# Attention and two feed-forward layers on one core: place of the scale products, tiles of the last weight load, shape of the last job

## The chip, the cores and the metric

The kernel runs on one core of one Trainium2 chip. The metric is the device time of one execution in microseconds; lower is better. Three runs of the kernel before were timed, and one more execution was profiled.

## The reference, cut to what matters

```python
mask = q_bucket[:, :, :, None] == k_bucket[:, :, None, :]      # 2 x 8 heads, 768 tokens, 64 wide
scores = np.where(mask, scale * q @ k.T, -1e9)
attn = softmax(scores)
x = (attn @ v)                       # as 1536 tokens x 512
p = domain_probs / domain_probs.sum(-1)
for e in range(4):                   # first feed-forward: 4 experts, 512 -> 1024 -> 512
    out += p[:, e:e+1] * (np.maximum(x @ w1[e], 0) @ w2[e])
h = out @ w_in                       # second feed-forward: 512 -> 2048 -> 512
g = np.where(h >= 1, h, np.where(h <= -1, 0, (h + 1) ** 2 / 4))
return g @ w_out
```

## The kernel before, in words

**Units of work.** Each expert is cut into two halves of 512 hidden columns, which gives the weight blocks u = 0 to 7; the second feed-forward has four such blocks, u = 8 to 11. A block has four chunks f of 128 hidden columns, for each of its two matrices (kind 1 and kind 2). A job is a pair of a block and a group of token tiles (128 tokens each). Its first layer makes 12 products per chunk into one PSUM tile; its second layer makes three products per chunk and token tile into one PSUM tile per token tile. Each operand is held as a high and a low half, so every product is made three times.

**First stage.** The attention is cut into 96 units, and 17 jobs on the first six token tiles (`JOBS_A`, L45) run between them. The list scheduler `Order` (L61 to L283) sets the order of this stage: every step has a cost, a due time and the buffers that it uses, and the scheduler writes out one order for all engines. `fill` (L893) lists the job steps. For each of the 52 weight chunks of either kind it has a load (`ldw`, `w_dma`, L803), on SP or on ACT's queue, whichever the scheduler finds free; a conversion on ACT (`whi`, L832); and two low halves on POOL or DVE (`wlo`, L836). A chunk is loaded into a raw tile, of which there are two for each kind (`raw_n`, L296), so chunk s can't be loaded before the low halves of chunk s - 2 are made. The last eight chunks (block 1, four of each kind) are converted here but used in the second stage. Where the scheduler foresees idle time on PE it puts in products on a dummy tile (`warm`, L1040), so many as fit. In one place of the stage the scale of block 0 is found: PE turns a column of maxima (L406), DVE takes four small steps (L394 to L404), PE spreads the result (L411).

**Second stage.** After `S.run` the attention's pools are closed (`attx.close()`), and new pools take their memory. From there the order is that of the code. The loop at the end makes, for each job and chunk, `l1b` (L1313) of the next job, one pending transposition of x (`x_all`), `step` (L1432), `l2b` (L1400) of this job, and `step` again. There are two PSUM tiles for the first layer (`mm_tile`), so a first layer waits for all readers of the tile two before it. `step` moves the generators on: loads that are due (`fetch_w`), scaling and conversion of weights (`w_steps`, `conv_w`), the scan of x after the first feed-forward (`x2_steps`), and the unpacking of the second feed-forward's weights (`w64_steps`). All of SP's loads in this stage are in one queue, in order; the first of them (L1193, L1195) stand at its start.

**Scale products.** A scale is found in `fin` (L1083): a maximum on DVE, a turn on PE, four steps on DVE (L1094 to L1097), a spread on PE, two steps on DVE (L1107, L1108). The two PE steps ride in the free columns 384 to 511 of a first-layer tile (`rider`, L1065), and `rest()` is the DVE part that reads them. In `l1b` `rest()` is the last thing.

**Blocks 8 to 11.** The first layer's result goes through two activations on ACT (L1350, L1351; the first tile is `ga`, the second `gg`), a product on DVE (L1352), a sum on POOL (L1353) and then `halves` (L1357 on ACT, L1358 on DVE). `halves` of a chunk is put off to the next chunk (`halve`, `split`). The activations need five small factors per token group, which `scales2` (L1296) makes in five DVE steps; it is called in `l1b` itself, at f = 0. The factors need the scale of the group's x (`e2`) and those of both weight matrices.

**The end.** `l2b_last` (L1414) makes the second layer of the last job: it first lets `split` make the last halves, then goes through the three token tiles one by one, with chunks 0 to 3 each, and each tile's sum goes to DVE (L1391) and out on SP (L1396).

Of the kernel before, what the change touches and what calls it, by code (L numbers as in the profile page):

```python
# [286 lines left out]
def attn_moe_kernel(ctx: ExitStack, tc, q, k, v, proj, probs, w1, w2, w_in, w_out, out):  # L287
# [510 lines left out]
    NCH = 4 * len(loads)  # L798
    wt = {1: {}, 2: {}}
# [4 lines left out]
    def w_dma(kind, s, e):  # L804
        if s >= NCH:
            return
        nxt_dma[kind] = s + 1
        u, f = loads[s // 4], s % 4
        if u >= 8:
            return  # L810
        t = raw[kind][s] = raw_p.tile([128, 512], F32, tag=f"raw{kind}", name=f"raw{kind}", bufs=raw_n[kind])
        if kind == 1:
            src = w1[u // 2]
            f0 = (u % 2) * 512
            src = src[:, f0 + f * 128:f0 + f * 128 + 128].rearrange("(c p) f -> p c f", p=128)
            e.dma_start(t.rearrange("p (c f) -> p c f", c=KC), src)
        else:
            src = w2[u // 2]
            f0 = (u % 2) * 512 + f * 128
            e.dma_start(t, src[f0:f0 + 128, :])  # L820
# [72 lines left out]
    def fill():  # L893

        NA = 4 * (job_load[len(JOBS_A) - 1] + 2)
        wb = {}
        half_raw = {}
        for s in range(NA):
            for kind in (1, 2):
                br = S.buf(f"raw{kind}", 2)  # L900
# [56 lines left out]
    with tc.manual_schedule():  # L957
# [347 lines left out]

        def grp(j):
            return jobs[j][1][0] // 3
# [5 lines left out]
        def l1b(j, f):  # L1313
# [26 lines left out]
            if u < 8:  # L1340
                act.activation(gg[:, 0:n], ps[:, 0:n], AF.Relu, scale=2.0 ** -15)  # L1341
                act.activation(hh[:, 0:n], gg[:, 0:n], AF.Copy)  # L1342
                dve.tensor_tensor(hl[:, 0:n], gg[:, 0:n], hh[:, 0:n], ALU.subtract)  # L1343
            else:
                need(2, u)
                if f == 0 and (u == 8 or grp(j) == 0):
                    scales2(u, slice(grp(j), grp(j) + 1) if u == 8 else slice(0, 4))
# [5 lines left out]
                pool.tensor_tensor(gg[:, 0:n], gg[:, 0:n], a[:, 0:n], ALU.add)  # L1353
                split()
# [6 lines left out]
            rest()  # L1361

        def l2b_mm(j, i, f, o):
            if j < JF:
                l2_mm(j, i, f, o)
                return
            whi, wlo = w16[2, jobs[j][0], f]
            hh, hl = hts[j, f]
            ts = slice(i * 128, i * 128 + 128)
            pe.matmul(o, hh[:, ts], whi, start=(f == 0), stop=False)  # L1370
            pe.matmul(o, hh[:, ts], wlo, start=False, stop=False)  # L1371
            pe.matmul(o, hl[:, ts], whi, start=False, stop=(f == 3))  # L1372

        def l2b_ev(j, i, o):
            u, tts = jobs[j]
            tt = tts[i]
            if j < JF:
                l2_ev(j, i, o)
            elif u < 8:
                sc = prk[u][:, tt:tt + 1]  # L1380
                if tt not in started:
                    started.add(tt)
                    dve.tensor_scalar(acc[tt], o, sc, None, ALU.mult)
                else:
                    dve.scalar_tensor_tensor(acc[tt], o, sc, acc[tt], ALU.mult, ALU.add)
            else:
                ko = k5[u][:, 4, grp(j):grp(j) + 1]
                if u == 8:
                    act.activation(acc[tt], o, AF.Copy, scale=ko)
                else:  # L1390
                    dve.scalar_tensor_tensor(acc[tt], o, ko, acc[tt], ALU.mult, ALU.add)  # L1391
            if u == 11:
# [4 lines left out]
                    out[r0:r0 + 128 * n, :].rearrange("(t c) d -> t c d", c=n)[:, tt - TT0[g]], acc[tt]  # L1397
# [16 lines left out]
        def l2b_last(j):  # L1414
            split()
            for i in range(len(jobs[j][1])):
                o = ps_m.tile([128, DM], F32, tag=f"o{i}", name=f"o{i}")
                for f in range(4):
                    l2b_mm(j, i, f, o)
                l2b_ev(j, i, o)  # L1420

        def x2_steps(tts):
# [7 lines left out]
            turn.extend((tt, s2[:, c]) for tt in tts)  # L1430

        def step(j):  # L1432
# [7 lines left out]
            for kind in (1, 2):  # L1440
                next(wgen[kind], None)
            if j > JF:
# [55 lines left out]
```

## Time and profile before

| what | value |
|---|---|
| runs | 1015.18, 1015.7, 1019.3 us; median 1015.7 |
| the profiled execution | 1014.5 us, of which the span on the core is 1012.4 |
| PE busy, in the span | 955.4 us (94%) |
| DVE, ACT, POOL busy | 724.2, 728.3, 360.4 us |
| granted TensorE clock, mean | 0.987 |
| chain that ended last | PE 67%, DVE 11%, ACT 10%, DMA 8% |

The span is cut by the order of the program: to about 423 us the first stage, from there the second, in which the second feed-forward begins at about 733 us. The time outside the span (2.1 us) is that of the start and the end of an execution. PE's busy time counts modelled ends of products that overlap, so idle time counts only from where the pipe has run empty.

### The profile page before, as it was taken

The page shows a single profiled execution, that of the slowest core. Times are in us where ns is not written, and L with a number is a line of the kernel's source. Part 1 is how long each engine was busy: PE and PEld are TensorE (multiplying, and loading weights), DVE is VectorE, ACT ScalarE, POOL GpSimd, SP SyncE. Part 2 cuts the span into 40 slices and gives each one's busy share as a digit, 9 for nine tenths or more (in the row PEclk, how much of TensorE's full clock was granted, in tenths as well). Part 3 has the DMA queues.
Part 4 walks back from the last instruction along what each step waited for, and adds up shares of the span by engine and source line. Part 5 has one row for each costly group of instructions (what it writes and reads, how often), then busy time and mean ns, then how long its engine had stood idle before and what let it go on. Part 6 is the DMA issues. An engine that isn't in the chain of part 4 may idle for free.

```text
span 1012.4 us, 19329 instructions
## 1 busy us (share of the span) xinstructions
PE 955.4 (94%) x6847; PEld 614.8 (61%) x6847; DVE 724.2 (72%) x1932; ACT 728.3 (72%) x1574; POOL 360.4 (36%) x397
## 2 busy tenths in 40 slices
PE   5568999999999999899999999999998999999998
PEld 2246888787888789785555555555544555555553
DVE  6998988899888884447665756655677777774654
ACT  6888897889888884357786777767776785656442
POOL 0332555554645654505110111104241353434221
PEclk9879999999999999999999999999999999999999
DMA  9799999999999885352433333110110111100012
GB/s 225 170 217 189 215 223 237 235 229 198 191 231 204 179 184 123 117 165 62 147 108 101 125 105 104 42 42 22 42 42 22 43 42 53 32 1 1 1 44 82
DMA packets 254753, 121.35 MB, mean 120 GB/s; under 512 B 180736, under 2 KB 239424, under 8 KB 254656
## 3 DMA queue, kind: packets, MB, share of 16 engines
q1 hardware_dynamic: 251296, 117.50, 49.4%
q10 hardware_dynamic: 3360, 2.62, 0.9%
q8 instruction: 53, 0.87, 0.4%
q14 instruction: 44, 0.36, 0.1%
HBM read 70.28 MB, written 3.15 MB: 73 GB/s over the span
## 4 chain that ended last, share of the span: by engine, by line
PE 67%; DVE 11%; ACT 10%; DMA 8%; issue 3%; SPq 1%; POOL 0%; ACTq 0%; DVEq 0%; POOLq 0%
PE mm L1334 7%; PE mm L1335 7%; PE mm L1336 7%; PE o L1370 6%; PE o L1372 6%; PE o L1371 6%; PE s L636 4%; DMA pt<-pn 3%; PE m L868 3%; DMA raw<-in_moe_w_dram 3%; PE m L850 3%; PE m L851 3%; PE m L852 3%; PE m L870 3%; PE m L869 3%
## 5 line engine op out<-in xcount | busy, mean ns | idle before, releaser
L686 POOL TENSOR_TENSOR pn<-e,pn 128x192 f16<-128x192 f32 (+3 forms) x165 | 138.3, 843 | 193.9 <-ACT pn L678 49.1
L1353 POOL TENSOR_TENSOR gg<-gg,ga 128x384 f32<-128x384 f32 x64 | 70.3, 1099 | 153.8 <-DVE ga L1352 150.5
L1343 DVE TENSOR_TENSOR hl<-gg,hh 128x384 f16<-128x384 f32 x72 | 42.9, 596 | 82.1 <-ACT hh L1342 82.0
L658 DVE CUSTOM_DVE_ANT_0 e<-s,mk,sc 128x768 f32<-128x768 f32 x96 | 96.9, 1010 | 2.3 <-ACT acc L716 0.6
L636 PE MATMUL s<-xk,xq 128*128 128x384 f16 (+1 forms) x384 | 81.7, 337 | 13.6 <-DVE usm L658 9.7
L1350 ACT ACTIVATE ga<-mm,half,k 128x384 f32<-128x384 f32 x64 | 42.6, 666 | 68.2 <-PE mm L1336 46.8
L850 PE MATMUL m<-x0h,w1h 128*128 128x256 f32 x304 | 91.5, 301 | 0.0
L671 ACT ACTIVATE e<-e,usm 128x768 f32<-128x768 f32 x96 | 89.3, 930 | 1.9 <-ACT acc L716 0.2
L851 PE MATMUL m<-x0l,w1h 128*128 128x256 f32 x304 | 86.1, 283 | 0.2 <-DVE sc L530 0.2
L852 PE MATMUL m<-x0h,w1l 128*128 128x256 f32 x304 | 86.0, 283 | 0.0
L678 ACT ACTIVATE pn<-e 128x768 f16<-128x768 f32 (+3 forms) x104 | 81.7, 786 | 4.6 <-DMA pt<-pn 4.4
L1352 DVE SCALAR_TENSOR_TENSOR ga<-ga 128x384 f32<-128x384 f32 x64 | 38.5, 601 | 62.8 <-ACT ga L1350 62.8
L1372 PE MATMUL o<-w2l,hl 128*128 128x512 f16 x216 | 82.0, 379 | 1.1 <-DVE hl L1358 1.1
L1370 PE MATMUL o<-w2l,hh 128*128 128x512 f16 x216 | 82.1, 380 | 0.0
L1371 PE MATMUL o<-w2l,hh 128*128 128x512 f16 x216 | 82.0, 379 | 0.0
L1358 DVE SCALAR_TENSOR_TENSOR hl<-gg,k,hh 128x384 f16<-128x384 f32 x64 | 59.9, 936 | 20.7 <-ACT hh L1357 20.5
L1370 PE MATMUL o<-w2h,hh 128*128 128x512 f16 x192 | 73.0, 380 | 0.0
L1372 PE MATMUL o<-w2h,hl 128*128 128x512 f16 x192 | 72.9, 379 | 0.0
L1371 PE MATMUL o<-w2h,hh 128*128 128x512 f16 x192 | 72.8, 379 | 0.0
L1372 PEld LDWEIGHTS <-hl 128*128 128x128 f16 x408 | 39.9, 98 | 49.7 <-DVE hl L1358 1.6
L1341 ACT ACTIVATE gg<-mm 128x384 f32<-128x384 f32 x72 | 34.7, 483 | 46.2 <-PE mm L1104 21.9
L868 PE MATMUL m<-w2h,hh 128*128 128x512 f32 x152 | 65.0, 428 | 0.0
(258 smaller groups left out, 2934.4 us busy)
## 6 DMA issues: line engine op xcount, KB each, us to landing
raw<-in_moe_w_dram SPq DMA_DIRECT2D x126, 256.0 KB, 3.4
r<-in_moe_w_in_dram SPq DMA_DIRECT2D x16, 512.0 KB, 3.7
r<-in_moe_w_out_dram SPq DMA_DIRECT2D x16, 512.0 KB, 3.5
rawx<-in_moe_w_dram SPq DMA_DIRECT2D x24, 256.0 KB, 3.9
out_dram<-acc SPq DMA_DIRECT2D x12, 256.0 KB, 2.0
raw<-in_moe_w_dram ACTq DMA_DIRECT2D x10, 256.0 KB, 3.0
w<-in_moe_w_dram SPq DMA_DIRECT2D x8, 256.0 KB, 5.2
rk<-in_k_dram SPq DMA_DIRECT2D x5, 384.0 KB, 3.8
```

What stands on the lines that cost most here:

```text
L636: pe.matmul(sps[:, j, 0:n], st["xq"][1 - i][:, hh * QG[pgs[m][0]][2] + c], st["x"][:, hh, 384 * j:384 * j + n], start=(i == 0), stop=(i == 1))
L658: dve.tensor_tensor_reduce(out=e.rearrange("p (a b) -> p a b", a=2), in0=u["s"][:, :, 0:384], in1=u["mk"].rearrange("p (a b) -> p a b", a= ...
L671: act.activation(u["e"], u["e"], AF.Exp, scale=-1.0, bias=sm[:, 2:3], accum_out=sm[:, 3:4])
L678: act.activation(u["pn"][:, c0:c1], u["e"][:, c0:c1], AF.Copy)
L686: eng[e].tensor_tensor(u["pn"][:, 768 + c0:768 + c1], u["e"][:, c0:c1], u["pn"][:, c0:c1], ALU.subtract)
L850: pe.matmul(ps[:, 0:n], hi[:, ws], xh[:, kc, xs], start=(kc == 0), stop=False)
L851: pe.matmul(ps[:, 0:n], hi[:, ws], xl[:, kc, xs], start=False, stop=False)
L852: pe.matmul(ps[:, 0:n], lo[:, ws], xh[:, kc, xs], start=False, stop=(kc == KC - 1))
L868: pe.matmul(o, hh[:, ts], whi, start=(f == 0), stop=False)
L1370: pe.matmul(o, hh[:, ts], whi, start=(f == 0), stop=False)
L1371: pe.matmul(o, hh[:, ts], wlo, start=False, stop=False)
L1372: pe.matmul(o, hl[:, ts], whi, start=False, stop=(f == 3))
```

## The change

There are four parts. In `fill` and `w_dma`, the last two chunks of each kind (s = 50 and 51) are loaded into tiles of the pool that held raw keys, values and queries (`rk`, `rv`, `rq`), under the scheduler's rules for these tags. In `l1b`, `rest()` stands right behind the first activation for blocks below 8, and behind the sum on POOL, ahead of `split`, for the others. The factors are made by a new function `factors`, called where the scan of x ends and in every `step`, as soon as their inputs are there, no more in `l1b`. In `l2b_last`, the first two token tiles go through chunks 0 to 2 before either goes through chunk 3, and the third token tile is made, evicted and sent in two halves of 256 columns.

```diff
--- before.py
+++ after.py
@@ -796,6 +796,8 @@
         job_load.append(len(loads) - 1)
         job_last.append(j == len(jobs) - 1 or jobs[j + 1][0] != u)
     NCH = 4 * len(loads)
+    NA = 4 * (job_load[len(JOBS_A) - 1] + 2)
+    EXTRA = {NA - 2: (("rk", 1), ("rq", 2)), NA - 1: (("rv", 1), ("rq", 2))}
     wt = {1: {}, 2: {}}
     raw = {1: {}, 2: {}}
     done_w = {1: 0, 2: 0}
@@ -808,7 +810,15 @@
         u, f = loads[s // 4], s % 4
         if u >= 8:
             return
-        t = raw[kind][s] = raw_p.tile([128, 512], F32, tag=f"raw{kind}", name=f"raw{kind}", bufs=raw_n[kind])
+        if s in EXTRA:
+            tag, n = EXTRA[s][kind - 1]
+            if n == 1:
+                t = flat(rq_p.tile([128, 2, 6, D], F32, tag=tag, name=tag, bufs=1))[:, 0:512]
+            else:
+                t = flat(rq_p.tile([128, 12, D], F32, tag=tag, name=tag, bufs=2))[:, 0:512]
+            raw[kind][s] = t
+        else:
+            t = raw[kind][s] = raw_p.tile([128, 512], F32, tag=f"raw{kind}", name=f"raw{kind}", bufs=raw_n[kind])
         if kind == 1:
             src = w1[u // 2]
             f0 = (u % 2) * 512
@@ -892,12 +902,11 @@
 
     def fill():
 
-        NA = 4 * (job_load[len(JOBS_A) - 1] + 2)
         wb = {}
         half_raw = {}
         for s in range(NA):
             for kind in (1, 2):
-                br = S.buf(f"raw{kind}", 2)
+                br = S.buf(*EXTRA[s][kind - 1]) if s in EXTRA else S.buf(f"raw{kind}", 2)
                 load(f"ldw{kind}.{s}", 0.73, lambda e, kind=kind, s=s: w_dma(kind, s, e), lambda cur: cur + K_LDW, w=[f"raw{kind}.{s}"],
                      use=[br], act_too=True, gate=4)
                 if s // 4 == NA0 + NA1 - 1:
@@ -1303,6 +1312,16 @@
             dve.reciprocal(cc, gp)
             dve.tensor_scalar(ko, gp, ew[2, u], None, ALU.mult)
 
+        have, e2_done = set(), set()
+
+        def factors(u, g):
+            if (u, g) in have or (1, u) not in scaled or (2, u) not in scaled:
+                return
+            gs = {g} if u == 8 else set(range(4))
+            if gs <= e2_done:
+                have.update((u, i) for i in gs)
+                scales2(u, slice(g, g + 1) if u == 8 else slice(0, 4))
+
         def grp(j):
             return jobs[j][1][0] // 3
 
@@ -1339,18 +1358,20 @@
             gg = g_p.tile([128, 384], F32, tag="gg", name="gg")
             if u < 8:
                 act.activation(gg[:, 0:n], ps[:, 0:n], AF.Relu, scale=2.0 ** -15)
+                rest()
                 act.activation(hh[:, 0:n], gg[:, 0:n], AF.Copy)
                 dve.tensor_tensor(hl[:, 0:n], gg[:, 0:n], hh[:, 0:n], ALU.subtract)
             else:
                 need(2, u)
-                if f == 0 and (u == 8 or grp(j) == 0):
-                    scales2(u, slice(grp(j), grp(j) + 1) if u == 8 else slice(0, 4))
+                factors(u, grp(j))
+                assert (u, grp(j)) in have
                 k2, kh, gp, cc, ko = (k5[u][:, i, grp(j):grp(j) + 1] for i in range(5))
                 a = g_p.tile([128, 384], F32, tag="ga", name="ga")
                 act.activation(a[:, 0:n], ps[:, 0:n], AF.Relu, bias=half, scale=kh)
                 act.activation(gg[:, 0:n], ps[:, 0:n], AF.Relu, bias=nhalf, scale=kh)
                 dve.scalar_tensor_tensor(a[:, 0:n], a[:, 0:n], 1.0, a[:, 0:n], ALU.min, ALU.mult)
                 pool.tensor_tensor(gg[:, 0:n], gg[:, 0:n], a[:, 0:n], ALU.add)
+                rest()
                 split()
 
                 def halves():
@@ -1358,20 +1379,19 @@
                     dve.scalar_tensor_tensor(hl[:, 0:n], gg[:, 0:n], cc, hh[:, 0:n], ALU.mult, ALU.subtract)
 
                 halve.append(halves)
-            rest()
-
-        def l2b_mm(j, i, f, o):
+
+        def l2b_mm(j, i, f, o, cs=slice(0, DM)):
             if j < JF:
                 l2_mm(j, i, f, o)
                 return
             whi, wlo = w16[2, jobs[j][0], f]
             hh, hl = hts[j, f]
             ts = slice(i * 128, i * 128 + 128)
-            pe.matmul(o, hh[:, ts], whi, start=(f == 0), stop=False)
-            pe.matmul(o, hh[:, ts], wlo, start=False, stop=False)
-            pe.matmul(o, hl[:, ts], whi, start=False, stop=(f == 3))
-
-        def l2b_ev(j, i, o):
+            pe.matmul(o, hh[:, ts], whi[:, cs], start=(f == 0), stop=False)
+            pe.matmul(o, hh[:, ts], wlo[:, cs], start=False, stop=False)
+            pe.matmul(o, hl[:, ts], whi[:, cs], start=False, stop=(f == 3))
+
+        def l2b_ev(j, i, o, cs=slice(0, DM)):
             u, tts = jobs[j]
             tt = tts[i]
             if j < JF:
@@ -1388,13 +1408,13 @@
                 if u == 8:
                     act.activation(acc[tt], o, AF.Copy, scale=ko)
                 else:
-                    dve.scalar_tensor_tensor(acc[tt], o, ko, acc[tt], ALU.mult, ALU.add)
+                    dve.scalar_tensor_tensor(acc[tt][:, cs], o, ko, acc[tt][:, cs], ALU.mult, ALU.add)
             if u == 11:
                 g = 0 if tt < 2 else (1 if tt < 6 else 2)
                 b, t0, n = QG[g]
                 r0 = b * S_ + t0
                 sp.dma_start(
-                    out[r0:r0 + 128 * n, :].rearrange("(t c) d -> t c d", c=n)[:, tt - TT0[g]], acc[tt]
+                    out[r0:r0 + 128 * n, :].rearrange("(t c) d -> t c d", c=n)[:, tt - TT0[g], cs], acc[tt][:, cs]
                 )
 
         def l2b(j, f):
@@ -1413,11 +1433,19 @@
 
         def l2b_last(j):
             split()
-            for i in range(len(jobs[j][1])):
-                o = ps_m.tile([128, DM], F32, tag=f"o{i}", name=f"o{i}")
+            u, tts = jobs[j]
+            o = [ps_m.tile([128, DM], F32, tag=f"o{i}", name=f"o{i}") for i in range(2)]
+            for i in range(2):
+                for f in range(3):
+                    l2b_mm(j, i, f, o[i])
+            for i in range(2):
+                l2b_mm(j, i, 3, o[i])
+                l2b_ev(j, i, o[i])
+            for h in range(2):
+                o = ps_m.tile([128, DM], F32, tag=f"o{2 * h}", name=f"o{2 * h}")
                 for f in range(4):
-                    l2b_mm(j, i, f, o)
-                l2b_ev(j, i, o)
+                    l2b_mm(j, 2, f, o[:, 0:256], slice(256 * h, 256 * h + 256))
+                l2b_ev(j, 2, o[:, 0:256], slice(256 * h, 256 * h + 256))
 
         def x2_steps(tts):
             g = tts[0] // 3
@@ -1428,6 +1456,8 @@
                 yield
             yield from fin(am, 3, e2[:, c], s2[:, c], 1)
             turn.extend((tt, s2[:, c]) for tt in tts)
+            e2_done.add(g)
+            factors(8, g)
 
         def step(j):
             for x in late:
@@ -1439,6 +1469,9 @@
             x2q[:] = [x for x in x2q if next(x, "end") != "end"]
             for kind in (1, 2):
                 next(wgen[kind], None)
+            for u in range(8, 12):
+                for g in range(4):
+                    factors(u, g)
             if j > JF:
                 w64_step()
 
```

The new order, where it matters below (line numbers of the new kernel stand 9 to 40 above those of the old one). First, ACT at the end of the first stage; `w1h` and `w2h` are the conversions of weight chunks, `hh<-mm` the first eviction of the second stage. Before:

```order
L832 ACTIVATE w1h<-raw_7500 128x512
L832 ACTIVATE w2h<-raw_7405 128x512
L832 ACTIVATE w2h<-raw_7413 128x512
L820 DMA raw_7553<-in_moe_w_dram 128x512
L832 ACTIVATE w2h<-raw_7550 128x512
L832 ACTIVATE w2h<-raw_7553 128x512
L857 ACTIVATE hh<-mm 128x256 x5
```

and now:

```order
L842 ACTIVATE w1h<-rv 128x512
L867 ACTIVATE hh<-m 128x256
L842 ACTIVATE w2h<-raw_7418 128x512
L842 ACTIVATE w2h<-raw_7437 128x512
L842 ACTIVATE w2h<-rq 128x512 x2
L867 ACTIVATE hh<-mm 128x256 x5
```

The load that stood between the conversions is gone from here, and the last two read a query tile.

Second, PE where the scale of block 0 is found in the first stage (`mx_w` is turned, `dmxw` is spread). Before:

```order
L406 MATMUL m<-ident,mx_w 2x128
L868 MATMUL m<-w2h,hh 128x512
L869 MATMUL m<-w2l,hh 128x512
L870 MATMUL m<-w2h,hl 128x512
...
L411 LDWEIGHTS ones
L411 MATMUL m<-dmxw,ones 128x2
```

and now:

```order
L406 MATMUL m<-ident,mx_w 2x128
L1049 LDWEIGHTS warm
L1049 MATMUL mm<-warm 128x256
...
L411 LDWEIGHTS ones
L411 MATMUL m<-dmxw,ones 128x2
L878 MATMUL m<-w2h,hh 128x512
```

Between the turn and the spread stood nine second-layer products; now six dummy products stand there, and the second layer comes behind the spread.

Third, DVE at the second token group of block 8 (`e` is the scale of x, `k` the factors, `mt` the first step on the next ridden product). Before:

```order
L1352 SCALAR_TENSOR_TENSOR ga<-ga 128x384
L1358 SCALAR_TENSOR_TENSOR hl<-gg,k_11111,hh 128x384
L1107 COPY e_7612<-mm 128x1
...
L1385 SCALAR_TENSOR_TENSOR acc<-o_11137,prk,acc 128x512
L1300 TENSOR_SCALAR k_11111<-e_7612,ew_8_10405 128x1
...
L1352 SCALAR_TENSOR_TENSOR ga<-ga 128x384
L1358 SCALAR_TENSOR_TENSOR hl<-gg,k_11111,hh 128x384
L1094 TENSOR_REDUCE mt<-mm 1x1
```

and now:

```order
L1372 SCALAR_TENSOR_TENSOR ga<-ga 128x384
L1116 COPY e_7614<-mm 128x1
L1117 RECIPROCAL s_7615<-mm 128x1
L1379 SCALAR_TENSOR_TENSOR hl<-gg,k_10883,hh 128x384
L1309 TENSOR_SCALAR k_10883<-e_7614,ew_8_10407 128x1
...
L1405 SCALAR_TENSOR_TENSOR acc<-o_11144,prk,acc 128x512
L1372 SCALAR_TENSOR_TENSOR ga<-ga 128x384
L1103 TENSOR_REDUCE mt<-mm 1x1
```

The copy of the scale moved ahead of the low half `hl`, the factors ahead of the three evictions `acc`, and the next ridden product's first step ahead of its `hl`. On SP, the loads of chunks 50 and 51 moved forward among the attention's transposes, and the order of the first stage differs on every engine from about SP's 177th row on. SP's first load of the second stage, which waited for no engine, now waits for POOL's last low half, because its tile lies over the query tiles.

## Rows read from the trace of the kernel before

**Rows 1.** Windows, by stage: PE, PEld, DVE, ACT, POOL busy us (instructions), clock, DMA, GB/s

```profile
290.00:423.00 133.00, 132.90 (x1259) 111.89 (x1257) 94.09 (x292) 95.92 (x227) 73.09 (x98) 1.00 0.77 163
423.00:437.00 14.00, 9.66 (x64) 9.33 (x65) 5.24 (x20) 3.08 (x8) 4.98 (x8) 0.88 0.93 299
...
700.00:800.00 100.00, 92.98 (x515) 49.35 (x514) 69.72 (x164) 71.12 (x143) 28.73 (x26) 1.00 0.13 40
```

**Rows 2.** Waits of PE, 395 to 450 us: total us, times, longest

```profile
PE mm L850 <- DVE hl L862: 3.6, 1, 3.6
PE mm L850 <- DVE acc L880: 0.8, 1, 0.8
```

**Rows 3.** Timeline of ACT at the end of the first stage: start, duration, what

```profile
424.51 0.35 ACTq L820 DMA_DIRECT2D raw<-in_moe_w_dram  x1
...
429.06 0.63 ACT L832 ACTIVATE w2h<-raw 128x512 fp32r<-128x512 f32 x1 [1.93 <-DMA raw<-in_moe_w_dram]
429.59 0.64 ACT L857 ACTIVATE hh<-mm 128x256 fp32r<-128x256 f32 x2
```

**Rows 4.** Timeline of POOL there

```profile
421.66 2.82 POOL L836 TENSOR_TENSOR w2l<-raw,w2h 128x256 fp32r<-128x256 f32 x4 [0.56 <-ACT w2h L832]
```

**Rows 5.** Timeline of DVE there: one step beside POOL's work, and without it

```profile
423.83 0.66 DVE L1262 TENSOR_TENSOR ex<-ex,ekv 128x1 f32<-128x1 f32 x1
...
425.91 0.16 DVE L1262 TENSOR_TENSOR ex<-ex,ekv 128x1 f32<-128x1 f32 x1
```

**Rows 6.** Timeline of PE behind that wait: two products, ten apart

```profile
431.28 0.42 PE L850 MATMUL mm<-x0h,w1h 128*128 128x256 f32 x1
...
433.41 0.41 PE L851 MATMUL mm<-x0l,w1h 128*128 128x256 f32 x1
```

**Rows 7.** Timeline of PE where the scale of block 0 is found

```profile
407.06 0.27 PE L406 MATMUL m<-ident,mx_w 128*2 128x128 f32 x1
...
409.32 0.17 PE L411 MATMUL m<-dmxw,ones 2*128 2x2 bf16 x1
```

**Rows 8.** Timeline of DVE there

```profile
407.37 0.28 DVE L394 TENSOR_REDUCE mxw<-m 2x1 f32<-2x128 f32 x1 [0.60 <-PE m L406]
...
408.59 0.32 DVE L404 TENSOR_SCALAR dmxw<-ident,mxw 2x2 bf16<-2x2 f32 x1
```

**Rows 9.** Waits of PE, 700 us to the end

```profile
PE mm L1334 <- DVE mt L1094: 3.7, 3, 2.6
PE mm L1334 <- DVE sw L1108: 1.8, 2, 1.6
PE mm L1334 <- ACT gg L1351: 1.3, 3, 0.6
PE o L1372 <- DVE hl L1358: 1.1, 1, 1.1
PE mm L1091 <- DVE mx L1088: 0.6, 1, 0.6
```

**Rows 10.** Timeline of DVE around the longest of these

```profile
756.62 2.06 DVE L1385 SCALAR_TENSOR_TENSOR acc<-o,prk,acc 128x512 f32<-128x512 f32 x3
...
760.85 1.07 DVE L1358 SCALAR_TENSOR_TENSOR hl<-gg,k,hh 128x384 f16<-128x384 f32 x1 [0.50 <-ACT hh L1357]
761.85 0.27 DVE L1094 TENSOR_REDUCE mt<-mm 1x1 f32<-1x128 f32 x1
```

**Rows 11.** Waits of ACT for the factors, whole span

```profile
ACT ga L1350 <- DVE k L1302: 12.7, 6, 3.5
```

**Rows 12.** Timeline of DVE at the end: the last eviction

```profile
1008.53 0.75 DVE L1391 SCALAR_TENSOR_TENSOR acc<-o,k,acc 128x512 f32<-128x512 f32 x1 [1.84 <-PE o L1372]
```

**Rows 13.** DMA issues of the page: KB each, median us from issue to landing

```profile
raw<-in_moe_w_dram SPq DMA_DIRECT2D x126, 256.0 KB, 3.4
...
out_dram<-acc SPq DMA_DIRECT2D x12, 256.0 KB, 2.0
```

**Rows 14.** Waits of SP's queue, 290 to 430 us; L691 are the attention's transposes

```profile
SPq L691 <- POOL pn L686: 33.8, 19, 3.4
```

## The prediction

> **What bounds the kernel now.** I read the windows first, then the waits of PE, then the timelines around each wait. In the last third of the first stage PE is busy 132.9 of 133 us at full clock, so there another engine's work costs nothing until it holds PE up. The next 14 us have only 9.7 us of PE, at a clock of 0.88, and from 700 to 800 us PE lacks 7 us again [rows 1]. The list of PE's waits says what is late. At the border of the stages it is the low halves `hl` on DVE, 3.6 us, and an eviction on DVE, 0.8 [rows 2]. From 700 us on the waits sum to 3.7 + 1.8 + 1.3 + 1.1 + 0.6 = 8.5 us, of which DVE's steps on the ridden scale products (`mt`, `sw`, `mx`) end 6.1 [rows 9]. So I look for these few places and take the rest of the span as PE's own work, which the change leaves as it is: the order shows the same products, but for three more dummies of 256 columns, some 0.1 us each.
>
> **Part 1, the last weight load in other tiles.** Before, ACT, which goes in order, issues the last load at 424.51, when POOL has given a raw tile free, and then stands at the conversion that needs it until 429.06; the first eviction of the second stage is behind it, at 429.59 [rows 3]. PE's 3.60 us wait is that chain: load, conversion, eviction, `hl`. Its second price is the clock. After the wait ten products of 256 columns start within 2.13 us, 0.213 each [rows 6], against some 0.12 at full clock (twice the columns' own time is 0.21). The 0.88 over 14 us are 1.7 us at most [rows 1], and fourteen products at the lower level cost 14 x 0.09 = 1.3. The place costs 0.84 + 3.6 + a little over 1 of clock, some 5.2 less what was natural of it: 5.1 at the most can come back.
>
> Now the load comes earlier, the last four conversions, 0.63 us each [rows 3], end near 423.7, and ACT is free for the eviction. What is late next is DVE. POOL's last low halves come in one train: four halves take 2.82 us from 421.66 [rows 4], and four more bring POOL to about 427.2. Beside POOL's work DVE's small two-operand step takes 0.66 us, after it 0.16 [rows 5]; there are four of them in the two groups of small steps that stand ahead of `hl`. With POOL busy to 427.2 the second pair is slow too, 1.0 us more, and the first `hl`, 0.42 us each, are ready near 428.4, where PE would want them at 426.7: a wait of 1.7 stays, and no more than a short dip of the clock. Gain 5.1 - 1.7 = **3.4**; bounds 2.5 (the dip costs its full 1 again) and 5.1 (nothing stays).
>
> The rule in the Trainium skill, SBUF — State Buffer, section "SBUF: two separate sides", is that DVE and GpSimd hold one pair of ports alternately, for a whole instruction, when a DVE step reads two SBUF operands. The rows agree (0.66 against 0.16). By the rule the 1.7 us stay; without it the wait would be about 0.7 and the sum 1.0 lower.
>
> Two covers can go. SP's first loads of the second stage now wait for POOL's last low half, 427.2 where they began near 424; a load lands 3.4 us after its issue [rows 13], so 430.6, and ACT's first conversion of it is due near 432. That costs nothing, with a little over 1 us to spare. And the loads of chunks 50 and 51 stand among the attention's transposes in SP's queue, which already waits for POOL there 33.8 us in 19 places without PE noticing [rows 14, 1]; cost nothing, while PE has other jobs' products ahead; the bound is the third rival.
>
> **What part 1 moves in the first stage.** The scheduler writes another order from SP's 177th row on. On one place I see a price: the turn and the spread of the scale of block 0 stood at 407.06 and 409.32 with nine products between them [rows 7], which covered DVE's four steps, 407.37 to 408.91 [rows 8]. Now only six dummies stand there, so PE earns nothing from the turn to the spread: the chain is 1.54 us, less the 0.42 of an `hl` that lay in it, plus the two starts of 0.3. I take **+1.5**; bounds 0.5 (DVE has nothing else in between and PE's next job hides a part) and 2.5 (another step lies in it). Elsewhere PE's list is the same in another order; I take 0, bounds -0.5 and +2.
>
> **Part 2 and 3, `rest()` earlier and the factors early.** They act together, so I cost them as one. The longest wait shows the chain: DVE evicts three sums from 756.62 for 2.06 us; only then come the five small steps of the factors, and ACT waits for them; the low half starts at 760.85 and takes 1.07, and only behind it stands `mt`, at 761.85 [rows 10]. PE waits 2.6 us for it [rows 9]. Now the factors stand ahead of the evictions and `mt` ahead of the low half. ACT's wait for factors, 12.7 us in 6 places [rows 11], goes, and with it what hung on it. Of PE's waits 3.7 + 1.8 + 1.3 + 0.6 = 7.4 us hang on this [rows 9], in 9 places; each has a drain of the pipe beside it, some 0.15 us (a product lasts about twice the distance of two starts [rows 6]), so 1.3 more: 8.7. What can stay: `mt` still needs the DVE steps ahead of it, product on `ga` (0.56) included, and ACT's `gg` is as late as ACT is loaded (71% in that window [rows 1]). I take 7.5, **-7.5**; bounds 3.5 (the ridden steps are read in time, all else moves to the next reader) and 9.
>
> **Part 4, the end.** PE's wait of 1.1 us for the last `hl` [rows 9] goes, as two tiles' chunks 0 to 2 (18 products, some 4 us) now stand ahead of it. The last eviction, 0.75 us for 512 columns [rows 12], becomes one of 256: 0.4 at the least, so 0.35 less. The last transfer is 128 KB for 256, which took 2.0 us from issue to landing [rows 13]: between 0 and 1.0 less. A load of the same size takes 3.4 in the rows beside it, so size is not all of it, and I take 0.3. The third tile has 24 products of 256 columns for 12 of 512; with some 0.02 us per start this gives back 0 to 0.3. Sum **-1.8**; bounds -1.1 and -2.2.
>
> **The sum.** -3.4 + 1.5 - 7.5 - 1.8 = -11.2 us. The profiled execution took 1014.5, so 1003.3; the median of the runs is 1.2 above the profiled one, so against the runs the forecast is **1004.5**. The best bounds give -5.1 + 0 - 9 - 2.2, about -16 or 999; the worst -2.5 + 4.5 - 3.5 - 1.1 = -2.6, or 1013. About 0.5%, 5 us, is what a measurement of this kernel can tell from no change.
>
> **Rivals.** First: the second stage gives half of it back. From 700 us DVE and ACT are both busy 70% [rows 1]; `rest()` ahead of `hl` makes each low half, and the second layer behind it, a microsecond later, and PE then waits for `hl` where it waited for `mt`. For it speaks that `hl` and `mt` use one engine; against it, that `halves` of blocks 8 to 11 are put off by a whole chunk. With 3.5 to 4 in place of 7.5: 1008. Chance 0.2.
>
> Second: the first stage takes back the gain at the border, or the change does not do what it says there: the scheduler's new order opens waits of PE between 290 and 423 us, where there were none, or the loads come as late as before. Then part 1 is worth 0 or +1 instead of -3.4 + 1.5 = -1.9: 1006.5 to 1009; I take 1008. Chance 0.15.
>
> Third, slower: SP's queue goes in order, and a load that waits for a tile holds every transpose behind it, by which PE's last attention products come. The rows show SP waiting up to 3.4 us in one place for POOL [rows 14]; the moved loads wait for tiles that the attention itself frees, so one such hold could last as long as the load and its step, some 6 us. It costs only when the work that PE has besides runs out; by the order, PE has some 26 us of other products behind the last attention step, 2 us less than before. So it decides from about three holds of this length on; each further one is 6 us on the path. With three such: 18 - 11.2, which is 1022. Chance 0.06.
>
> **How the numbers follow.** The forecast has what is left, 0.59, and spreads from 1000 to 1008 by its own bounds. The range, 999 to 1011, leaves out the third rival and the ends of the others, under 0.2. Faster by over 0.5% means below 1010.6: the forecast and most of both smaller rivals, 0.86. Within 0.5%: the worse ends of these, 0.08. Slower: the third rival, 0.06.
>
> **What would show it.** In the changed trace: ACT's first `hh` near 424 to 427 instead of 429.6, PE's wait there below 2 us, the clock after it near full. The turn and the spread about 2 us apart with only dummies between. No wait of PE for `mt`, `sw` or `mx` from 700 us on, and none of ACT for `k`; DVE's `mt` ahead of `hl`. At the end no wait for `hl`, and a last eviction of some 0.4 us. The prediction is wrong if new waits of PE stand between 290 and 423 us, if PE waits for `hl` of blocks 8 to 11, or if the border still holds PE for 3 us or more.

## The result, and the profile after

The changed kernel took 1004.73 us (median of 6 runs, 1003.01 to 1008.56) against 1015.44 before (6 runs, 1012.8 to 1019.3): a ratio of 0.9894, interval 0.9866 to 0.9923, 10.7 us less. Measured once more beside other kernels it took 1004.96, ratio 0.988 (0.9854 to 0.9906). The forecast was 1004.5.

The profiled execution took 1004.35 us, its span is 1002.6. The windows of the changed kernel by stage, with the columns of [rows 1]:

```profile
290.00:423.00 133.00, 131.85 (x1256) 111.24 (x1255) 97.42 (x295) 97.28 (x233) 69.31 (x87) 1.00 0.76 168
423.00:437.00 14.00, 11.75 (x82) 10.56 (x81) 7.59 (x22) 5.06 (x10) 5.60 (x8) 1.00 0.44 132
...
700.00:800.00 100.00, 98.44 (x550) 53.37 (x549) 72.40 (x175) 78.42 (x156) 32.68 (x29) 1.00 0.13 38
```

The window at the border holds 2.1 us more of PE's work and the clock stays at 1.00; from 700 to 800 us 5.5 us of PE's idle time are gone; but PE lost 1 us in the stretch that was full before. PE's waits, 280 to 450 us, as in [rows 2]:

```profile
PE mm L860 <- DVE hl L872: 1.4, 1, 1.4
PE m L411 <- DVE dmxw L404: 1.0, 1, 1.0
PE mm L860 <- DVE acc L890: 0.8, 1, 0.8
```

and from 700 us to the end, as in [rows 9], where 8.5 us stood:

```profile
PE mm L1100 <- DVE mx L1097: 0.6, 1, 0.6
PE mm L1353 <- DVE sw L1117: 0.6, 1, 0.6
PE mm L1353 <- DVE mt L1103: 0.4, 1, 0.4
```

Cutting both spans at the same instructions of PE gives the account (us; before, after): to the start of the first stage's last second-layer product 422.51, 424.90 (+2.39); from there to the first `o` product of the second stage, "the border" from here on, 13.78, 10.19 (-3.59); to the last first-layer product, "the second stage", 560.86, 553.74 (-7.12); to the end of the last product 11.34, 10.07 (-1.27); to the end of the span 3.87, 3.66 (-0.21). The sum is -9.8, the difference of the spans.

### The profile page after: what moved, and what is told of

The parts are those of the page before. It is cut to its first block, busy times and chain, and to the rows that moved or that the text cites. A ratio compares the mean times of both kernels' runs of the same rounds, so it can differ in the third digit from the quotient of the medians.

```text
span 1002.6 us, 19362 instructions
## 1 busy us (share of the span) xinstructions
PE 955.0 (95%) x6862; PEld 617.5 (62%) x6862; DVE 731.1 (73%) x1935; ACT 729.3 (73%) x1580; POOL 358.5 (36%) x387
## 5 line engine op out<-in xcount | busy, mean ns | idle before, releaser
L658 DVE CUSTOM_DVE_ANT_0 e<-s,mk,sc 128x768 f32<-128x768 f32 x96 | 96.8, 1009 | 2.0 <-ACT acc L716 0.2
L1390 PE MATMUL o<-w2l,hh 128*128 128x512 f16 (+1 forms) x220 | 82.7, 376 | 0.0
L1391 PE MATMUL o<-w2l,hh 128*128 128x512 f16 (+1 forms) x220 | 82.5, 375 | 0.0
L1392 PE MATMUL o<-w2l,hl 128*128 128x512 f16 (+1 forms) x220 | 82.5, 375 | 0.0
```

The source lines that it names most:

```text
L658: dve.tensor_tensor_reduce(out=e.rearrange("p (a b) -> p a b", a=2), in0=u["s"][:, :, 0:384], in1=u["mk"].rearrange("p (a b) -> p a b", a= ...
L1390: pe.matmul(o, hh[:, ts], whi[:, cs], start=(f == 0), stop=False)
L1391: pe.matmul(o, hh[:, ts], wlo[:, cs], start=False, stop=False)
L1392: pe.matmul(o, hl[:, ts], whi[:, cs], start=False, stop=(f == 3))
```

## The experiments

Each of the twelve runs was timed with the kernel before beside it. Since the parts are small, each is also read from its trace by the same cuts. For the first stage the cut, "the stretch" from here on, is from the attention's 64th exponential on ACT (near 266 us, the program is the same up to there) to the last product: the time to that exponential alone ranges from 265.1 to 268.5 over the fourteen profiled executions, more than most parts are worth. Of the +2.39 above, 0.60 lies ahead of that mark and is chance.

### Each part alone

The edits are the four pieces of the diff above, each put into the kernel before by itself.

Part 1, the tiles:

```diff
...
+    EXTRA = {NA - 2: (("rk", 1), ("rq", 2)), NA - 1: (("rv", 1), ("rq", 2))}
...
```

> The kernel before with part 1 alone (the last weight chunks in freed tiles). My theory, from the markers of the two traces: the last second-layer product of the first stage starts 2.4 us later (422.5 to 424.9), and from there to the first `o` product of the second stage takes 3.6 us less (13.8 to 10.2); the span is then about 1.2 us shorter than before, near 1011, a ratio of 0.997 to 1.000. Rival: the 2.4 us later first stage is chance of one execution, and part 1 is worth the full 3.6 us, a ratio near 0.996; then the gap between the turn and the spread of block 0's scale is short here too. The place between 700 us and the end stays as before: waits of PE for `mt` and `sw` of 5 us or so, shifted.

Measured: 1015.6 us, ratio 1.0001 (0.9984 to 1.0018): no gain. The border did take 10.19, but the first stage's stretch took 157.97 us where the five executions in the old order took 155.54 to 156.73. The second stage, which part 1 does not touch, took 562.38, 1.5 us more than in [rows 1]'s execution. The clock says why; windows around the longest wait [rows 10], part 1 alone:

```profile
756.00:762.00 6.00, 3.39 (x16) 1.45 (x15) 4.89 (x15) 4.10 (x10) 1.27 (x2) 0.92 0.00 0
762.00:768.00 6.00, 6.00 (x29) 3.29 (x28) 3.12 (x6) 2.92 (x6) 1.00 (x1) 0.80 0.01 3
```

and the kernel before, the same two windows:

```profile
756.00:762.00 6.00, 3.57 (x21) 1.84 (x19) 5.00 (x14) 4.34 (x11) 2.52 (x2) 1.00 0.09 37
762.00:768.00 6.00, 5.82 (x35) 3.43 (x36) 4.68 (x11) 3.54 (x9) 1.00 (x1) 1.00 0.01 3
```

The same wait of 2.6 us was followed by full clock in one execution and by a clock of 0.80 in the other. That is a mean of the two levels, 2.4 and 1.2 GHz; over the two windows it takes 1.7 us of PE's clock (6 x 0.08 + 6 x 0.20), about the 1.5 us that the stage is longer.

Part 2, `rest()`:

```diff
                 act.activation(gg[:, 0:n], ps[:, 0:n], AF.Relu, scale=2.0 ** -15)
+                rest()
...
+                rest()
                 split()
...
-            rest()
```

> The kernel before with part 2 alone (`rest()` ahead of the low half). Theory: the ridden steps are read about 1 us earlier, but ACT still waits for the factors (12.7 us in 6 places before), so the waits for `mt` and `sw` (5.5 us) shrink to a half: 2.5 to 4 us less than before, a ratio of 0.996 to 0.998. Rival: part 2 does nearly all of the 7.1 us, and the wait for the factors was covered; then the ratio is 0.993.

Measured: 1009.96 us, ratio 0.9938 (0.9915 to 0.9961). In the trace the second stage took 557.07, 3.8 less, as the theory had it. The timed ratio speaks for the rival: its 0.993 lies in the interval, and of the theory's 0.996 to 0.998 only the edge does (4.0 to 8.6 us less). The 7.1 us are not in the trace, but it is one execution; the two readings disagree, and this is left open.

Part 3, the factors:

```diff
...
-                if f == 0 and (u == 8 or grp(j) == 0):
-                    scales2(u, slice(grp(j), grp(j) + 1) if u == 8 else slice(0, 4))
+                factors(u, grp(j))
...
```

> The kernel before with part 3 alone (factors made early). Theory: ACT's wait for factors goes, and with it the largest of PE's waits (2.6 us at 759 us) becomes about 1; `mt` still stands behind the low half. 3 to 4 us less, a ratio of 0.996 to 0.997. Rival: the low half ahead of `mt` is what PE waits for, and the factors alone give under 1.5 us.

Measured: 1014.78 us, ratio 0.9994 (0.9977 to 1.0011). The theory falls, the rival holds: ACT waits no more for a factor, and PE still waits 3.7 us for `mt`. DVE there, part 3 alone (three evictions, `ga`, low half, `mt`):

```profile
758.25 2.06 DVE L1395 SCALAR_TENSOR_TENSOR acc<-o,prk,acc 128x512 f32<-128x512 f32 x3
760.24 0.56 DVE L1362 SCALAR_TENSOR_TENSOR ga<-ga 128x384 f32<-128x384 f32 x1
761.31 1.07 DVE L1368 SCALAR_TENSOR_TENSOR hl<-gg,k,hh 128x384 f16<-128x384 f32 x1 [0.51 <-ACT hh L1367]
762.30 0.27 DVE L1094 TENSOR_REDUCE mt<-mm 1x1 f32<-1x128 f32 x1
```

With part 2 alone:

```profile
757.34 2.05 DVE L1386 SCALAR_TENSOR_TENSOR acc<-o,prk,acc 128x512 f32<-128x512 f32 x3
759.32 0.20 DVE L1300 TENSOR_SCALAR k<-e,ew 128x1 f32<-128x1 f32 x1
...
760.50 0.56 DVE L1353 SCALAR_TENSOR_TENSOR ga<-ga 128x384 f32<-128x384 f32 x1 [0.43 <-ACT ga L1351]
761.07 0.28 DVE L1094 TENSOR_REDUCE mt<-mm 1x1 f32<-1x128 f32 x1
```

and with both, in the changed kernel:

```profile
753.73 2.06 DVE L1405 SCALAR_TENSOR_TENSOR acc<-o,prk,acc 128x512 f32<-128x512 f32 x3
755.73 0.56 DVE L1372 SCALAR_TENSOR_TENSOR ga<-ga 128x384 f32<-128x384 f32 x1
756.29 0.28 DVE L1103 TENSOR_REDUCE mt<-mm 1x1 f32<-1x128 f32 x1
```

From the end of the evictions to `mt` it is 2.0 us with part 3, 1.7 with part 2 (3.2 before [rows 10]) and 0.5 with both. Each part alone leaves DVE standing once for ACT: with part 3 at the low half, which waits for `hh`; with part 2 at `ga`, which waits for the activation that waits for `k`. In the traces the second stage is 3.8 us shorter with part 2, 0.1 with part 3 and 7.1 with both. Part 3's 0.1 has a fall of the clock in it, to 0.72 in the window 762 to 768 us, which the kernel before has not; it takes at most 1.7 us (6 x 0.28), so without it part 3 would be worth up to 1.8.

Part 4, the end: `l2b_last` and the `cs` arguments as in the diff above.

> The kernel before with part 4 alone (the end in another order and in halves). Theory: from the last first-layer product to the end 1.5 us less, as in the changed kernel (15.2 to 13.8 us), a ratio of 0.9985. Rival: the end's gain needs the earlier `hl` of parts 2 and 3; then a wait for `hl` of 0.5 us or more stays in front of the last second layer.

Measured: 1012.41 us, ratio 0.9972 (0.9955 to 0.9989). From the last first-layer product to the last product's end 10.07 for 11.34, the changed kernel's value, and no wait of PE for `hl` is left: the part stands by itself.

### Parts 2 to 4 without part 1

> The changed kernel without part 1 (parts 2, 3 and 4 on the kernel before). Theory: the second stage takes 553.7 us and the end 10.1 as in the changed kernel, the border some 13 us with a clock below full behind it, and the first stage some 1.7 us less than in the changed kernel; so 1 to 1.5 us above the changed kernel, near 1006, a ratio of 0.989 to 0.992. Rival: part 1 alone measured no gain, so it is worth nothing, and this kernel is at the changed kernel's time or below it.

Measured: 1005.03 us, ratio 0.9901 (0.9878 to 0.9924), with the first stage at 155.54, the border at 12.91, the second stage at 553.74, the end at 10.07. The ratio lies in the theory's range too, and the difference to the changed kernel, 0.3 us (2 us by its second measurement), is below the intervals, so this run alone does not decide. Part 1 alone does, narrowly: its interval, 1.6 us less to 1.8 more, leaves out the 1.9 us that the prediction gave it. So the rival stands: part 1 is worth nothing that can be measured.

The timed gains of part 2, part 3 and part 4 alone are 6.3, 0.6 and 2.8 us, 9.7 in sum, and 10.1 together. So the runs do not show that parts 2 and 3 give more together than apart; with intervals of some 2 us each they do not exclude the traces' difference either.

### What holds the border now

The three sums of `x_bound` written so that each step reads one tensor:

```diff
-            dve.tensor_tensor(e, v[0], v[1], ALU.add)
-            dve.tensor_tensor(e, e, v[2], ALU.add)
-            dve.tensor_tensor(e, e, v[3], ALU.add)
+            dve.tensor_scalar(e, v[0], v[1], None, ALU.add)
+            dve.tensor_scalar(e, e, v[2], v[3], ALU.add, ALU.add)
```

> The changed kernel, with the three sums of `x_bound` written so that each reads one tensor and takes the other values as per-partition scalars (same sums, one step fewer per group). Theory, that the two-operand step waits for POOL's step: in the changed kernel four such steps at the border take 0.65 to 0.67 us and end where a POOL half ends, so the new form takes about 0.15 each beside a busy POOL; the two groups shrink from 4.3 us to about 2.2, the first `hl` ends near 428.7 instead of 430.2 and PE's wait of 1.4 us there is gone; 1.4 us less than the changed kernel's span for the border (10.2 to 8.8 us). [...] Rival: any DVE step beside POOL is held for the rest of POOL's step; then the new steps take 0.6 too and the wait stays above 1 us.

Measured: 1004.15 us, ratio 0.9898 (0.9874 to 0.9921). The border took 8.52 for 10.19, and no wait of PE for `hl` is left there. In the changed kernel POOL and DVE stand so (POOL's two trains of halves, then DVE's sums and the first `hl`):

```profile
424.05 2.82 POOL L846 TENSOR_TENSOR w2l<-raw,w2h 128x256 fp32r<-128x256 f32 x4 [2.11 <-ACT w2h L842]
426.82 2.82 POOL L846 TENSOR_TENSOR w2l<-rq,w2h 128x256 fp32r<-128x256 f32 x4
```

```profile
426.00 0.19 DVE L1270 TENSOR_TENSOR ex<-ekv,ekv 128x1 f32<-128x1 f32 x1
426.22 0.67 DVE L1271 TENSOR_TENSOR ex<-ex,ekv 128x1 f32<-128x1 f32 x1
426.92 0.66 DVE L1272 TENSOR_TENSOR ex<-ex,ekv 128x1 f32<-128x1 f32 x1
...
428.13 0.16 DVE L1270 TENSOR_TENSOR ex<-ekv,ekv 128x1 f32<-128x1 f32 x1
428.32 0.66 DVE L1271 TENSOR_TENSOR ex<-ex,ekv 128x1 f32<-128x1 f32 x1
429.02 0.65 DVE L1272 TENSOR_TENSOR ex<-ex,ekv 128x1 f32<-128x1 f32 x1
```

The long steps end at 426.89 and 427.58; POOL's halves, 0.7 us each, end at 426.87 and 427.57. L1270 reads two tensors as well and is short both times; it began just before a half ended (426.17 and 428.27) and ended just behind it. Now, beside the same POOL train (427.2 to 432.8 in this execution):

```profile
429.39 0.27 DVE L1271 TENSOR_SCALAR ex<-ex,ekv,ekv 128x1 f32<-128x1 f32 x1
...
430.44 0.27 DVE L1271 TENSOR_SCALAR ex<-ex,ekv,ekv 128x1 f32<-128x1 f32 x1
...
431.48 0.42 DVE L872 SCALAR_TENSOR_TENSOR hl<-mm,hh 128x256 fp32r<-128x256 f32 x1
```

Two tensors from SBUF wait for POOL's step; one tensor with per-partition scalars took 0.20 and 0.27 beside it, so it does not. The rule of the Trainium skill (SBUF — State Buffer, "SBUF: two separate sides") is that a DVE step with two SBUF inputs and a POOL step that reads SBUF take a shared pair of ports in turn, each for its whole instruction. The trace agrees. The 1.7 us do not show in the time: the ratio, 0.9898 against 0.9894, moved by less than the intervals. In the profiled execution the stretch took 160.19, which leads to the next group.

### The first stage

The price that was forecast is there. PE in the changed kernel between the turn and the spread, as in [rows 7]:

```profile
407.82 0.81 PE L1049 MATMUL mm<-warm 128*128 128x256 bf16 x6
409.67 0.16 PE L411 MATMUL m<-dmxw,ones 2*128 2x2 bf16 x1 [1.03 <-DVE dmxw L404]
```

Its cause can be undone: the scheduler had put the scans of three chunks on ACT, ahead of the conversions.

```diff
-                    tk(f"scan{i}", dict(act=0.81, dve=0.6), lambda e, kind=kind, s=s, i=i: w_scan(e, half_raw.setdefault((kind, s), raw[kind].get(s)), i),
+                    tk(f"scan{i}", dict(dve=0.6), lambda e, kind=kind, s=s, i=i: w_scan(e, half_raw.setdefault((kind, s), raw[kind].get(s)), i),
```

> The changed kernel, with the scans of block 0's chunks allowed on DVE alone (the scheduler put three of them on ACT, ahead of the conversions, so that POOL's low halves and with them the second layer came too late to stand between the turn and the spread of the scale). Theory: nine products stand between them again, the six dummies and the wait of 1.0 us go, and the first stage is 1.5 to 1.9 us shorter, within what one execution's first stage varies (420.9 to 424.6 in four executions of one order). The rest as in the changed kernel. Rival: the scans on DVE hold back the evictions there, and new waits of PE for DVE above 1 us stand between 290 and 423 us.

Measured: 1004.78 us, ratio 0.9901 (0.988 to 0.9922). Nine products stand between the two steps and the wait is gone, but the stretch took 160.31: PE waits 1.4 us for a transpose near 296 us and 0.5 for a step of the softmax. No gain; the rival's kind of result, by another engine than it named.

Both edits together:

> Both edits together on the changed kernel. Theory: they lie at different places, so their gains add: about 3 us less than the changed kernel, near 1001.5, a ratio to the kernel before of 0.985 to 0.988. Rival: the timed difference to the changed kernel is under 1 us, since the first stage varies by more than the edits give.

> The changed kernel with scans on DVE and the one-tensor sums, once more. Theory: border 8.5 us again; the median 1 to 2.5 us below that of the changed kernel measured beside it. Rival: the 2.3 us of the first measurement were mostly the first stage's variation, and the two now agree within 1 us.

Measured: 1002.42 us, ratio 0.9871 (0.9849 to 0.9893), and again 1002.56, ratio 0.9859 (0.9831 to 0.9888): twice 2.3 to 2.4 us below the changed kernel's median, with a border of 8.53 and a stretch of 158.13 and 157.92. The intervals overlap the changed kernel's, so "faster than it" is likely and not settled; it is faster than the kernel before by 13 to 15 us.

> The changed kernel once more, beside the two others on one chip, since the parts differ by less than one execution's first stage does. Theory: ratio to the kernel before within its first interval, 0.987 to 0.992, PE's second stage 553.7 us and border 10.2 again. Rival: the first result was a favourable draw, and the ratio is above 0.992.

Measured: 1004.96, as expected in ratio, border (10.20) and second stage (553.75). But the stretch of the first stage took 161.29, with this wait of PE, which the first profiled execution of the same kernel doesn't have:

```profile
296.38 0.23 PE L706 MATMUL s<-vs,pt 128*128 128x64 f16 x1 [1.39 <-DMA pt<-pn]
```

Behind it the clock fell. The window around it, here and in the first profiled execution (columns of [rows 1]):

```profile
292.00:304.00 12.00, 10.52 (x83) 7.58 (x79) 7.66 (x29) 8.31 (x22) 3.21 (x4) 0.86 0.92 158
```

```profile
292.00:304.00 12.00, 11.91 (x127) 9.02 (x126) 10.55 (x36) 10.70 (x27) 4.40 (x4) 1.00 1.03 211
```

The fall takes up to 1.7 us (12 x 0.14), so wait and fall make up some 3.1 of the 3.9 us between the two executions of one kernel.

Two more orders. Chunk 51 alone in freed tiles, with the one-tensor sums:

```diff
-    EXTRA = {NA - 2: (("rk", 1), ("rq", 2)), NA - 1: (("rv", 1), ("rq", 2))}
+    EXTRA = {NA - 1: (("rv", 1), ("rq", 2))}
```

> The changed kernel with chunk 51 alone in freed tiles (chunk 50 in the ordinary raw tiles again) and the sums of `x_bound` in the one-tensor form. The order has twelve products between the turn and the spread of block 0's scale, and no dummies there. Theory: the border stays at 8.5 us as with both chunks moved, and the first stage, from the 64th exponential of the attention to its last product, is back at 155.5 to 156.7 us, against 157.4 to 160.3 in the orders with both chunks moved; the sum is 1.8 us less than scan_dve_xb's typical, a median near 1001 and a ratio to the kernel before of 0.984 to 0.988. Rival: chunk 50 now comes as late as before, its low half waits for it, and the border keeps a wait of 1 us or more for `hl`.

Measured: 1004.69 us, ratio 0.9874 (0.9847 to 0.9902), border 10.34, stretch 159.50 and not 155.5 to 156.7. The rival holds at the border: chunk 50 comes as late as it did, and ACT stands for it.

```profile
430.18 0.63 ACT L842 ACTIVATE w2h<-raw 128x512 fp32r<-128x512 f32 x1 [4.29 <-DMA raw<-in_moe_w_dram]
```

Both chunks, but held back until the 75th unit, with the one-tensor sums:

```diff
...
-                     use=[br], act_too=True, gate=4)
+                     use=[br], act_too=True, gate=75 if s in EXTRA else 4)
```

> The changed kernel with the loads of chunks 50 and 51 held until the attention's 75th unit has begun (a gate on the scheduler's load steps), and the one-tensor sums of `x_bound`. In its order nine second-layer products stand between the turn and the spread of block 0's scale, and the conversions of the last chunks still stand in one train ahead of the first eviction. Theory: what part 1 cost in the first stage came from loading chunk 50 at about 290 us, ahead of transposes and with another order behind it; so the first stage from the 64th exponential to its last product is back at 155.5 to 156.7 us, no wait of PE for a transpose above 0.5 us near 296 us, the border 8.5 us; together some 3 us less than the changed kernel, a median near 1001.5 and a ratio to the kernel before of 0.984 to 0.988. Rival: any new order of this stage costs 1 to 3 us somewhere, as the planner's costs are not the chip's; then the stretch is 157 us or more, with waits of PE that the kernel before does not have.

Measured: 1002.96 us, ratio 0.9858 (0.9827 to 0.9888); border 8.53; nine products stand between turn and spread. The stretch took 159.66 all the same, not 155.5. PE's waits, 290 to 450 us:

```profile
PE m L597 <- DMA xk<-nk: 1.9, 2, 1.6
PE s L706 <- DMA pt<-pn: 1.1, 1, 1.1
PE mm L860 <- DVE acc L890: 0.8, 1, 0.8
```

The 1.1 us near 297 us lie where the order of every engine is still that of the kernel before: the first difference stands on SP at 309.9 us, in the changed kernel at 289.3. So a late transpose there can come by chance. Of the eight executions with the load moved to about 290 us seven have such a wait after 290 us, of 0.5 to 1.6 us at the longest; of the five in the old order one has it, of 0.2. Behind four of the seven, with waits of 1.2 to 1.6 us, the clock fell to 0.86 in the window 292 to 304 us, and these four have the stretches of 159.5 to 161.3; the other four of the eight took 157.4 to 158.1 at full clock, one of them with a wait of 1.4. How much of the waits the moved load causes stays open.

## Why the prediction was right

**The total** was right, and its three gains came by the steps given and near in size. One price, that of the first stage, was taken too small, so that the total fits as closely as it does, 0.2 us, is in part luck.

**Part 1 at the border.** Forecast -3.4 with a wait of 1.7 us left, caused by two-operand steps beside POOL; measured -3.59, a wait of 1.4, by just these steps, and shown by taking them away. The terms of its ceiling, 0.84 + 3.6 + a little over 1, make some 5.5 and not 5.2, and the 0.84 did not go, since PE still waits 0.8 for the eviction; yet the ceiling of 5.1 is near what can be had, 5.26 with the one-tensor sums (13.78 to 8.52). The old order's border, 12.66 to 13.78 in five executions, puts the typical gain at 2.9. A dip of the clock after the rest of the wait did not come. SP's loads behind POOL's last half went out at 429.67 and no wait of PE for weights follows, so that cover held.

**Part 1 in the first stage** is where one term was too small: "Elsewhere PE's list is the same in another order; I take 0". The +1.5 for turn and spread is right in place and near in size (six dummies of 0.81 and a wait of 1.03 make 1.8). But the stretch took 157.4 to 161.3 us in the four executions with this order, 159.2 on average, against 155.9 for the old one: +3.3, not +1.5. Taking the waits for transposes (0, 0.8, 1.4 and 1.2 us) and the two falls of the clock (1.7 each) out of the four leaves +1.6, so the term itself was right and the rest, 1.7, came at the place that was put at 0; this is a subtraction, no run has taken them away. The cover that the prediction counted on, other jobs' products, did not help at 296 us, where the attention's product stood next in PE's order. By its own sign, new waits of PE between 290 and 423 us, this part of the prediction was wrong. With the border's 2.9 nothing is left of part 1, where 1.9 us were forecast, and the timing of part 1 alone agrees. The second rival named this outcome (its sum gives 1006.4 to 1007.4, not up to 1009) and the third a transpose held on SP, at 1.4 us instead of 18; the runs show the waits and leave their cause open.

**Parts 2 and 3.** Forecast -7.5, measured -7.12; 1.6 us of waits remain, where its signs had none: 0.6 of it at `mx`, the first step of `fin`, which the change does not move. Costing the two as one was sound, since in the traces each alone leaves DVE standing once for ACT. PE did not begin to wait for `hl` (first rival), since its readers come a chunk later.

**Part 4.** Forecast -1.8, measured -1.27 - 0.21 in this pair of traces. From the last product to the end of the span one execution varies: 3.86 to 4.31 with the old end in four traces, 3.25 to 3.66 with the new one in ten, 0.58 less on average, which makes -1.85. The wait went, the eviction of 256 columns took 0.48 and the transfer 1.7:

```profile
998.94 0.48 DVE L1411 SCALAR_TENSOR_TENSOR acc<-o,k,acc 128x256 f32<-128x256 f32 x1 [0.83 <-PE o L1392]
```

```profile
out_dram<-acc SPq DMA_DIRECT2D x2, 128.0 KB, 1.7
```

against 0.75 and 2.0 [rows 12, 13]; each gain came within 0.1 us. The forecast's own 0 to 0.3 that the smaller products would give back was not taken off in its -1.8. No run shows its 0.02 us per start: in the changed kernel products of 256 columns start 0.109 us apart and those of 512 0.216, so next to nothing was given back.

**Why the sum still fits.** The traces add to -9.8, the medians to -10.7 and, in the second measurement, -12.2, though part 1 lacks 1.9 us. The clock can make this good: long waits that the old kernel has cost an extra in some executions (1.5 us in the one shown under part 1), while its profiled execution had such a fall at the border only. The runs bear this out in part. The mean granted clock is 0.985 over 62 runs of the kernel before and 0.987 over 12 of the changed one, which is up to 2.8 us of the span; in the two profiled executions it is 0.987 and 0.986, so their difference has none of it. Another 0.4 us lie outside the span (2.16 and 1.79 us in the median of these runs). Which waits the clock's part comes from was seen in single executions only and is argued, not shown.

## What to carry to other kernels

Two steps that wait for each other across engines are best moved and costed together: in the traces each alone left an engine standing (3.8 us, and 0.1 with a fall of the clock in it), both together gave 7.1; the timed runs are too coarse to confirm the difference. Where a planner writes the order, an edit's local gain has to be set against a whole new order, and the stretch timed from a common mark over several executions, since a single one varied by 4 us here, most of it one wait and the fall of the clock behind it. A small step on DVE that must run beside POOL is best written with one tensor and per-partition scalars.

## What was not expected of the hardware

The same wait of PE, 2.6 us at 760 us, was followed by a granted clock of 0.80 and 0.72 in two executions and by 1.00 in two others (the kernel before and part 4 alone); behind the border's waits of 2.6 to 3.6 us the window 423 to 437 us was at 0.88 in all five executions in the old order, behind 1.4 us at 1.00. In the first stage waits of PE of 1.2 to 1.6 us near 296 us were followed by 0.86 (292 to 304 us) in four executions, one of 1.4 us by 1.00. A step of one element per partition with two tensors took 0.65 to 0.67 us beside POOL, 0.20 and 0.27 when written for one tensor with scalars.
